# Output rows 16 partitions apart, one output transfer, and fewer, larger transfers for the last V, w4 and wo

## Chip, cores, metric

One core of one Trainium2 chip. The metric is device microseconds (us) of one execution, the median of several. A profile is taken of one execution of a kernel; its span is about 1.8 us shorter than the time (1333.3 us for a time of 1335.15).

## The reference

A decode step for two batches, one position each: attention over a cache of 16384 positions and 32 heads, mixed by a gate with a small MLP block.

```python
# A_x (2,1,1024); k_cache, v_cache (2,32,16384,128); everything bfloat16
q = (x @ wq).reshape(B, 1, 32, 128)
p = softmax(q . k_cache * 128 ** -0.5)           # per batch and head
a = (p . v_cache).reshape(B, 1, 4096) @ wo       # wo (4096, 1024)
# ... x1 = x + (w1, w2 part of the MLP)
b = x1 + gelu(layernorm(x1) @ w3) @ w4           # w4 (3584, 1024)
return g * a + (1 - g) * b                       # g = sigmoid(sum(x * gate_w))
```

K and V alone are 537 MB (2 x 2 x 32 x 16384 x 128 elements of 2 bytes), so the step is mostly a matter of reading HBM.

## The kernel before

Everything that is large comes through a ring of three 64 KB-per-partition buffers: K and V in 32 tiles each of 8.4 MB (two heads of one batch), the weights between them. All these loads are issued on the queue of SP, each as soon as a buffer is free. After the last V come w4 and wo, cut into pieces so that the matmuls can follow the landing:

```python
V_SPLIT_LAST = [NJ // 2, NJ // 2]        # the last V in two halves
W4_SPLIT = [7] * 4                       # 28 rows of 1024 per partition
WO_SPLIT = [4] * 6 + [2, 2, 1, 1, 1, 1]  # 32 rows per partition

def load_pieces(key, weights, split):
    # ...
    for n in split:
        nc.sync.dma_start(out=t[:, r0 : r0 + n, :], in_=src[:, r0 : r0 + n, :])
        r0 += n
```

One "row" here is one row of 1024 elements in each of the 128 partitions, 256 KB in all. The products of w4 and wo add up in one PSUM tile. Four groups of 32 partitions each hold a quarter of the 1024 output columns; in each group the two batches are in the first two partitions:

```python
def group(g):
    return slice(32 * g, 32 * g + B)              # B = 2

def add_row_product(actT, w_row, last=False):     # one row: four matmuls
    for g in range(NQ):                           # NQ = 4, QW = 256
        nc.tensor.matmul(out_acc[group(g), :], lhsT=actT,
                         rhs=w_row[:, g * QW : (g + 1) * QW],
                         start=False, stop=last, skip_group_check=True)
# ... at the very end
rows = t_tile([P, QW], BF16)
nc.vector.tensor_copy(out=rows[:], in_=out_acc[:])
for b, queue in enumerate((nc.sync, nc.scalar)):  # one transfer for each batch
    queue.dma_start(out=out[b].rearrange("s (g n) -> (s g) n", g=NQ),
                    in_=rows[b : 96 + b + 1 : 32, :])
```

The rows of w2 are loaded in three transfers: six rows per partition over all partitions, 216 rows into 12 partitions in a pattern whose slowest dimension is 3 (`WAYS, QUAD, BASE, MORE = 3, 4, 6, 18`), and the remaining 40.

## Time and profile before

| | |
|---|---|
| time, median of 3 | 1334.81 us (1334.72 to 1334.83) |
| span of the profile | 1333.3 us |
| read from HBM | 572.53 MB, 429 GB/s over the span |
| DMA engines busy | nine tenths or more in all slices but the last |
| PE, DVE busy | 60%, 57% |

From the page of the profile of the kernel before; each digit is the busy share of the 16 DMA engines in one fortieth of the span, in tenths:

```profile
span 1333.3 us, 11505 instructions
...
DMA  9999999999999999999999999999999999999998
...
HBM read 572.53 MB, written 0.00 MB: 429 GB/s over the span
```

The loads hardly pause: nine tenths of the engines' time or more in all slices but the last. An engine elsewhere that waits costs nothing unless its wait delays an issue by so long that the queue runs dry, so the time is the length of the stream plus what has to happen after its last byte. Both parts of the change act at the end, which the timeline shows. Its columns are start, duration, engine, line, operation, tiles, count, and in brackets the idle time before and what ended it:

```profile
1285.55 3.64 PE L446 MATMUL O<-Vn,PT 128*32 128x512 bf16 x32
...
1292.49 3.64 PE L446 MATMUL O<-Vn,PT 128*32 128x512 bf16 x32 [3.30 <-DMA Vn<-in_A_v_cache_dram]
...
1305.37 1.67 PE L495 MATMUL out_acc<-w,h2T 128*2 128x256 bf16 x28 [2.58 <-DMA w<-in_B_w_dram]
...
1309.61 1.66 PE L495 MATMUL out_acc<-w,h2T 128*2 128x256 bf16 x28 [2.57 <-DMA w<-in_B_w_dram]
...
1312.04 1.03 PE L495 MATMUL out_acc<-wo,Q 128*2 128x256 bf16 x16 [0.77 <-DMA wo<-in_A_wo_dram]
...
1314.47 1.02 PE L495 MATMUL out_acc<-wo,Q 128*2 128x256 bf16 x16 [1.40 <-DMA wo<-in_A_wo_dram]
...
1328.14 0.38 PE L495 MATMUL out_acc<-wo,Q 128*2 128x256 bf16 x4 [0.24 <-DMA wo<-in_A_wo_dram]
...
1328.78 0.39 PE L495 MATMUL out_acc<-wo,Q 128*2 128x256 bf16 x4 [0.25 <-DMA wo<-in_A_wo_dram]
...
1329.42 0.38 PE L495 MATMUL out_acc<-wo,Q 128*2 128x256 bf16 x4 [0.26 <-DMA wo<-in_A_wo_dram]
...
1329.85 0.42 DVE L703 CAST T<-out_acc 128x256 bf16<-128x256 f32 x1 [29.71 <-PE out_acc L495]
1330.30 0.63 SPq L705 DMA_DIRECT2D out_dram<-T  x1
1330.31 0.61 ACTq L705 DMA_DIRECT2D out_dram<-T  x1
```

PE is ahead of the loads at every step: each block of matmuls is short, and was released by a landing. Hence the starts of the blocks are the times of the landings, and their distances are what a transfer costs when the queue is full. Seven rows take 4.24 us (1309.61-1305.37), four take 2.43, one takes 0.64. Two of these give the price: a row costs (4.24-0.64)/6 = 0.60 us, and a transfer 0.64-0.60 = 0.04 us more, whatever the number of rows (all these transfers go to 128 partitions). Four rows should then take 2.44, and 2.43 were measured.

The chain of waits (start, duration, what) names the same end:

```profile
1319.55 9.83 DMA wo<-in_A_wo_dram
1329.38 0.04 issue
1329.42 0.41 PE out_acc L495 x4
1329.83 0.02 issue
1329.85 0.42 DVE T L703
```

The last row is issued 9.83 us before it lands. Its issue had to wait for an earlier piece, but the queue in front of it was full all that time, so that wait cost nothing.

### The profile page before, as it was taken

The page shows a single profiled execution, that of the slowest core. Times are in us where ns is not written, and L with a number is a line of the kernel's source. Part 1 is how long each engine was busy: PE and PEld are TensorE (multiplying, and loading weights), DVE is VectorE, ACT ScalarE, POOL GpSimd, SP SyncE. Part 2 cuts the span into 40 slices and gives each one's busy share as a digit, 9 for nine tenths or more (in the row PEclk, how much of TensorE's full clock was granted, in tenths as well). Part 3 has the DMA queues.
Part 4 walks back from the last instruction along what each step waited for, and adds up shares of the span by engine and source line. Part 5 has one row for each costly group of instructions (what it writes and reads, how often), then busy time and mean ns, then how long its engine had stood idle before and what let it go on. Part 6 is the DMA issues. An engine that isn't in the chain of part 4 may idle for free.

```text
span 1333.3 us, 11505 instructions
## 1 busy us (share of the span) xinstructions
PE 805.6 (60%) x4982; PEld 354.5 (27%) x5045; DVE 759.7 (57%) x1001; ACT 27.2 (2%) x68; POOL 12.8 (1%) x40
## 2 busy tenths in 40 slices
PE   2577655766556755556665555566655556665564
PEld 1223222332225322222222222222222222222231
DVE  1677665475652665555666555566655556666540
ACT  0000000000000000000000000000000000000000
POOL 0000000000000000000000000000000000000000
PEclk9788777787777777788887777888777788877775
DMA  9999999999999999999999999999999999999998
GB/s 410 439 437 433 423 437 431 427 434 431 439 428 441 431 423 437 441 437 425 433 437 431 433 433 437 433 431 437 435 429 433 437 437 425 435 435 433 431 421 337
DMA packets 12377, 573.27 MB, mean 430 GB/s; under 512 B 1384, under 2 KB 1392, under 8 KB 2203
## 3 DMA queue, kind: packets, MB, share of 16 engines
q1 hardware_dynamic: 12313, 572.53, 99.4%
q8 instruction: 39, 0.64, 0.2%
q14 instruction: 11, 0.09, 0.0%
q10 hardware_dynamic: 14, 0.01, 0.0%
HBM read 572.53 MB, written 0.00 MB: 429 GB/s over the span
## 4 chain that ended last, share of the span: by engine, by line
PE 31%; DVE 30%; DMA 23%; another core or an unknown queue 12%; issue 2%; ACT 1%; ACTq 0%; SPq 0%; DVEq 0%
DVE T L388 23%; PE S L402 20%; DMA Kn<-in_A_k_cache_dram 13%; PE O L446 7%; DMA wt<-in_B_w_dram 4%; DMA Vn<-in_A_v_cache_dram 3%; DMA wo<-in_A_wo_dram 3%; PE misc L255 2%; DVE Os L461 2%; ACT Pr L430 1%; DVE PT L434 1%; PE misc L604 1%; PE misc L585 1%; DVE mx L423 1%
## 5 line engine op out<-in xcount | busy, mean ns | idle before, releaser
L402 PE MATMUL S<-T,z 128*128 128x512 bf16 x1985 | 583.6, 423 | 323.7 <-DVE T L388 304.5
L388 DVE STREAM_TRANSPOSE T<-Kn 128x1024 f32<-128x1024 f32 x512 | 612.0, 1229 | 252.5 <-DMA Kn<-in_A_k_cache_dram 199.1
L402 PEld LDWEIGHTS <-z 128*128 128x128 bf16 x2048 | 211.2, 104 | 682.8 <-issue 521.5
L446 PE MATMUL O<-Vn,PT 128*32 128x512 bf16 x2048 | 121.4, 390 | 3.3 <-DMA Vn<-in_A_v_cache_dram 3.3
L446 PEld LDWEIGHTS <-PT 128*32 128x32 bf16 x2048 | 74.3, 140 | 49.2 <-issue 20.4
L457 DVE TENSOR_SCALAR Os<-O,xmask 128x128 f32<-128x128 f32 x32 | 11.2, 351 | 101.3 <-PE O L446 101.3
L255 PE MATMUL misc<-rs,ones_f 128*128 128x2 f32 x64 | 17.9, 350 | 79.1 <-DVE rs L477 79.1
L430 ACT ACTIVATE Pr<-S,nb 128x512 bf16<-128x512 f32 x32 | 22.0, 687 | 1198.9 <-DVE nb L425 1161.1
L469 PE MATMUL misc<-asel,Os 128*128 128x2 f32 x64 | 12.4, 264 | 50.9 <-DVE Os L461 50.9
L413 DVE TENSOR_REDUCE m<-S 128x1 f32<-128x512 f32 x32 | 22.1, 692 | 36.9 <-PE S L402 36.9
L434 DVE STREAM_TRANSPOSE PT<-Pr 128x512 bf16<-128x512 bf16 x32 | 22.8, 711 | 28.7 <-ACT Pr L430 28.7
L255 PEld LDWEIGHTS misc<-rs,ones_f 128*128 128x128 f32 x64 | 16.2, 314 | 83.9 <-issue 81.2
L461 DVE SCALAR_TENSOR_TENSOR Os<-O,xmask,Os 128x128 f32<-128x128 f32 x96 | 33.7, 351 | 3.4
L469 PEld LDWEIGHTS misc<-asel,Os 128*128 128x128 f32 x64 | 9.7, 192 | 65.2 <-DVE Os L461 61.0
L255 PE MATMUL misc<-mdiag,ones_f 128*128 128x128 f32 x64 | 15.5, 325 | 17.1 <-DVE mdiag L416 17.1
L423 DVE TENSOR_REDUCE mx<-misc 64x1 f32<-64x64 f32 x64 | 14.2, 222 | 19.1 <-PE misc L255 18.7
L362 POOL TENSOR_TENSOR z<-qsel,own 128x32 bf16<-128x32 bf16 x32 | 10.7, 333 | 1197.9 <-PE S L402 1168.1
L604 PE MATMUL misc<-xn2T,wt 128*128 128x2 bf16 x224 | 14.4, 202 | 8.0 <-DMA wt<-in_B_w_dram 8.0
L481 DVE RECIPROCAL rinv<-misc 128x2 f32<-128x2 f32 x32 | 5.5, 171 | 22.7 <-PE misc L255 22.7
L703 DVE CAST T<-out_acc 128x256 bf16<-128x256 f32 x1 | 0.4, 425 | 29.7 <-PE out_acc L495 29.7
L604 PEld LDWEIGHTS <-wt 128*128 128x128 bf16 x224 | 14.3, 169 | 8.2 <-DMA wt<-in_B_w_dram 8.2
L484 DVE SCALAR_TENSOR_TENSOR OT<-misc,g_bc,rinv 128x2 bf16<-128x2 f32 x32 | 7.0, 220 | 15.6 <-PE misc L469 15.6
(90 smaller groups left out, 122.3 us busy)
## 6 DMA issues: line engine op xcount, KB each, us to landing
Vn<-in_A_v_cache_dram SPq DMA_DIRECT2D x2, 4096.0 KB, 42.8
wt<-in_B_w_dram SPq DMA_DIRECT2D x1, 7168.0 KB
w<-in_B_w_dram SPq DMA_DIRECT2D x4, 1792.0 KB, 31.6
wo<-in_A_wo_dram SPq DMA_DIRECT2D x6, 1024.0 KB, 34.1
wt<-in_B_w_dram SPq DMA_DIRECT2D x1, 2048.0 KB, 37.3
wt<-in_B_w_dram SPq DMA_DIRECT2D x1, 1536.0 KB, 40.9
wo<-in_A_wo_dram SPq DMA_DIRECT2D x2, 512.0 KB, 18.8
wo<-in_A_wo_dram SPq DMA_DIRECT2D x4, 256.0 KB, 13.7
```

What stands on the lines that cost most here:

```text
L255: nc.tensor.matmul(ps[:], lhsT=ones_f[:], rhs=src, start=True, stop=True)
L388: moved = nc.vector.transpose(out=T[:].rearrange("p w j s -> p j w s"), in_=Kw[:, m * CW : (m + 1) * CW].rearrange("p (j w e) -> p j w e", ...
L402: nc.tensor.matmul(S[:], lhsT=z[:, v, NM - 1 - m : NM - 1 - m + P], rhs=Tb[:, v // 2, :, v % 2], start=(m == 0 and v == 0), stop=(m == NM ...
L413: nc.vector.reduce_max(out=m[:], in_=S[:], axis=AX.X)
L423: nc.vector.reduce_max(out=mx[pa, :], in_=mall[pa, pa], axis=AX.X)
L430: nc.scalar.activation(out=Pr[:], in_=S[:], func=ACTF.Exp, bias=nb[:], scale=scale, accum_out=rs[:])
L434: nc.vector.transpose(out=PT[:], in_=Pr[:])
L446: nc.tensor.matmul(O[32 * g : 32 * g + 32, :], lhsT=PT[:, m : CJ * 32 : 16], rhs=V[:, j0 : j0 + 4, :], start=(m == 0), stop=(m == NM - 1),)
L461: nc.vector.scalar_tensor_tensor(out=Os[:], in0=Ox, scalar=xmask[:, x : x + 1], in1=Os[:], op0=ALU.mult, op1=ALU.add,)
L469: nc.tensor.matmul(oc[:], lhsT=Os[:], rhs=asel[:], start=True, stop=True)
L585: nc.tensor.matmul(ps[group(g), :], lhsT=actT[rows, r, :], rhs=w[rows, r, g * HW : (g + 1) * HW], start=False, stop=(n == len(slots) - 1), ...
L604: nc.tensor.matmul(ps[:, c, :], lhsT=w[:, r, :].rearrange("k (p c) -> k p c", c=C)[:, :, c], rhs=actT[:, r, :], start=(r == 0), stop=(r == ...
```

## The change

The intent: the rows of the two batches are put 16 partitions apart, so that all eight output rows (4 groups x 2 batches) lie at one stride and leave in a single transfer, and the last loads are cut into fewer, larger pieces: 10 in place of 18. To have the second batch 16 columns on, the weights of the products get 17 columns with zeros between, which costs a memset and writes at a stride in three places, and for w4 (`h2`) a copy that was not there before.

```diff
-    V_SPLIT_LAST = [NJ // 2, NJ // 2]
# ... load_v: the last V in one transfer, as the others
-    W4_SPLIT = [7] * 4
-    WO_SPLIT = [4] * 6 + [2, 2, 1, 1, 1, 1]
+    W4_SPLIT = [14, 14]
+    WO_SPLIT = [8, 8, 8, 4, 2, 1, 1]
# ...
+    APART = 16
+    def apart(shape, dtype):
+        t = t_tile(shape + [APART * (B - 1) + 1], dtype)
+        nc.vector.memset(t[:], 0.0)
+        return t
+    def rows_of(g):
+        return slice(32 * g, 32 * g + APART * (B - 1) + 1)
     def add_row_product(actT, w_row, last=False):
         for g in range(NQ):
             nc.tensor.matmul(
-                out_acc[group(g), :],
+                out_acc[rows_of(g), :],
# ... the same in start_out; res, Q and h2 are made by apart() and filled with [:, :, ::APART]
-    for b, queue in enumerate((nc.sync, nc.scalar)):
-        queue.dma_start(
-            out=out[b].rearrange("s (g n) -> (s g) n", g=NQ), in_=rows[b : 96 + b + 1 : 32, :]
-        )
+    nc.sync.dma_start(
+        out=out.rearrange("b s (g n) -> g (b s) n", g=NQ), in_=rows[0 : P : APART, :]
+    )
```

More of the change, by code (lines that the diff above doesn't have):

```diff
@@ L114, in load_v @@
         t = big_tile("Vn")
-        tv = t[:].rearrange("p (j d) -> p j d", d=Dh)
-        src = cache_rows(A_v_cache, i)
-        j0 = 0
-        for n in V_SPLIT_LAST if i == NT - 1 else [NJ]:
-            nc.sync.dma_start(out=tv[:, j0 : j0 + n, :], in_=src[:, j0 : j0 + n, :])
-            j0 += n
+        nc.sync.dma_start(
+            out=t[:].rearrange("p (j d) -> p j d", d=Dh), in_=cache_rows(A_v_cache, i)
+        )
         vn_tiles[i] = t
@@ L506, in start_out @@
             zero_rows(out_acc, g, QW)
-        res = const.tile([P, KC, B], FP32, name="cen")
-        nc.vector.tensor_tensor(out=res[:], in0=x1, in1=over_r(omg_bc[:]), op=ALU.mult)
+        res = apart([P, KC], FP32)
+        nc.vector.tensor_tensor(
+            out=res[:, :, ::APART], in0=x1, in1=over_r(omg_bc[:]), op=ALU.mult
+        )
         for c in range(KC):
@@ L511, in start_out @@
                 nc.tensor.matmul(
-                    out_acc[group(g), c:QW:KC],
+                    out_acc[rows_of(g), c:QW:KC],
                     lhsT=res[:, c, :],
@@ L527, in wo_stage @@
         nc.tensor.matmul(q_ps[:], lhsT=perm[:], rhs=Q1[:], start=True, stop=True)
-        Q = const.tile([P, B, 32], BF16)
-        nc.vector.tensor_copy(out=Q[:], in_=q_ps[:])
+        Q = apart([P, 32], BF16)
+        nc.vector.tensor_copy(out=Q[:, :, ::APART], in_=q_ps[:].rearrange("p b r -> p r b"))
         wo = wt.pop("wo")
         for r in range(32):
-            add_row_product(Q[:, :, r], wo[:, r, :], last=(r == 31))
+            add_row_product(Q[:, r, :], wo[:, r, :], last=(r == 31))
     def layernorm(src, dst):
@@ L650, in st_down @@
         w4 = wt.pop("w4")
+        h2 = apart([P, FC], BF16)
+        nc.vector.tensor_copy(out=h2[:, :, ::APART], in_=h2T[:])
         for r in range(FC):
-            add_row_product(h2T[:, r, :], w4[:, r, :])
+            add_row_product(h2[:, r, :], w4[:, r, :])
     extra = {
@@ L703 @@
     nc.vector.tensor_copy(out=rows[:], in_=out_acc[:])
-    for b, queue in enumerate((nc.sync, nc.scalar)):
-        queue.dma_start(
-            out=out[b].rearrange("s (g n) -> (s g) n", g=NQ), in_=rows[b : 96 + b + 1 : 32, :]
-        )
+    nc.sync.dma_start(
+        out=out.rearrange("b s (g n) -> g (b s) n", g=NQ), in_=rows[0 : P : APART, :]
+    )
 _INS = ['A_x', 'A_k_cache', 'A_v_cache', 'A_wq', 'A_wo', 'B_x', 'B_w1', 'B_w2', 'B_w3', 'B_w4', 'gate_w']
```

## The prediction

> **What bounds the kernel.** The page's DMA row stands at nine tenths or more in every slice but the last (8); 572.53 MB come from HBM at 429 GB/s over the 1333.3 us span. The kernel is one stream of loads; PE (60%) and DVE (57%) have room. What the change does to them in mid-kernel (a memset and wider weights for the residual, near 267 us) is hidden while loads stay queued. Only the length of the stream and what follows its last byte count.
>
> **The tail before.** In the timeline the matmuls on w4 start as pieces land: 1301.13, 1305.37, 1309.61 us (7 rows, 4.24 apart); those on wo at 1312.04, 1314.47, 1316.89 (4 rows, 2.43 apart); the last at 1328.14, 1328.78, 1329.42 (1 row, 0.64 apart). So a row costs (4.24-0.64)/6 = 0.60 us and a transfer 0.04 us. From 1322 us the DMA moves about 300 GB/s, not 430: the packets show four of 16 engines finished, while twelve last to 1329. The cutting doesn't cause that; I expect it to stay. The DMA queue's waits for earlier pieces (8.6 us in the wo issues) cost nothing: the last issue, at 1319.55, is 9.83 us ahead of its landing.
>
> After that landing (1329.38): four matmuls 0.41, cast 0.42, two output issues at 1330.30 (0.63 on SP, 0.61 on ACT; an undisturbed load issue takes 0.33), end 1333.3.
>
> **What the change does.**
> 1. Eight transfers fewer (18 to 10 from the last V on): 8 x 0.04 = about 0.35 us off the stream, all on the critical path. No bytes are saved. The Trainium skill ("DMA: Bandwidth & Descriptors", Anatomy of one DMA) gives a single DMA about 2 us of fixed cost, mostly completion latency; with the queue full it overlaps, and 0.04 us agrees with its remark that the semaphore write is almost free.
> 2. The last V feeds PE whole: 64 matmuls (3.64 us per 32 at the tail's clock of 0.50) from 1292.4 to about 1299.8, 3.6 us later. The second w4 piece lands near 1309.5 and needs 3.3 us, the first wo piece near 1314.2: hidden.
> 3. Wider weights (17 columns for 2), two memsets, strided copies: under 2 us of DVE, hidden. An 8-row wo piece needs 2.05 us of PE against 4.8 us between landings; the last pieces are still single rows.
> 4. One output transfer of eight 512 B rows for two of four. The two issues seem to disturb each other; SP's landed 0.28 us after ACT's. Alone I expect 0.3 us less, between none and 0.5.
>
> **Predicted**: 1334.81 - 0.35 - 0.3 = 1334.15 us, range 1333.0 to 1335.1. Faster by over 2%: 0.01; within 2%: 0.98; slower by over 2%: 0.01.
>
> **What the profile would show.** Step 1: last wo landing near 1329.0 (before 1329.38), 8-row pieces about 4.85 us apart. Step 2: the last V's matmuls as one block of 7.3 us; no wo product waits for PE. Step 3: the last row product starts at its landing and takes 0.4 us. Step 4: one issue of about 0.35 us, and 2.6 to 2.9 us from its start to the span's end (3.0 before).
>
> **What would make it wrong.** An instruction fetch (16 KB, about 0.9 us on one DMA engine) falling on the slowest engine rather than another, up to 1 us either way; the transposes' buffers, now shared with the residual, delaying a load so far that the queue drains near 270 us; a slower descriptor pattern for the output; PE ordered so that w4's products hold up wo's.

## The result

Ratios in this document are the mean time of one kernel's runs over that of the other's of the same rounds, so they are not quite the ratios of the medians that are quoted.

| | before | after |
|---|---|---|
| median of 6 | 1334.72 us (1334.65 to 1334.83) | 1334.23 us (1334.12 to 1334.47) |
| ratio, 95% interval | | 0.9996 (0.9983 to 1.0009) |

The interval contains 1. Still, the slowest of the six runs after is faster than the fastest of the six before. The medians differ by 0.49 us; 0.65 were predicted.

From the page of the profile after:

```profile
span 1332.4 us, 11498 instructions
...
DMA  9999999999999999999999999999999999999998
...
HBM read 572.53 MB, written 0.00 MB: 430 GB/s over the span
```

The timeline after, the same places:

```profile
1292.13 5.94 PE L442 MATMUL O<-Vn,PT 128*32 128x512 bf16 x64 [7.09 <-DMA Vn<-in_A_v_cache_dram]
...
1309.25 3.16 PE L502 MATMUL out_acc<-w,T 128*17 128x256 bf16 x56 [5.32 <-DMA w<-in_B_w_dram]
...
1314.09 1.89 PE L502 MATMUL out_acc<-wo,T 128*17 128x256 bf16 x32 [1.68 <-DMA wo<-in_A_wo_dram]
...
1318.93 1.89 PE L502 MATMUL out_acc<-wo,T 128*17 128x256 bf16 x32 [2.95 <-DMA wo<-in_A_wo_dram]
...
1328.21 0.29 PE L502 MATMUL out_acc<-wo,T 128*17 128x256 bf16 x4 [0.22 <-DMA wo<-in_A_wo_dram]
...
1328.84 0.29 PE L502 MATMUL out_acc<-wo,T 128*17 128x256 bf16 x4 [0.34 <-DMA wo<-in_A_wo_dram]
...
1329.18 0.42 DVE L714 CAST T<-out_acc 128x256 bf16<-128x256 f32 x1 [28.02 <-PE out_acc L502]
1329.63 0.66 SPq L715 DMA_DIRECT2D out_dram<-T  x1
```

Each block of row products is still released by a landing, so PE is still ahead. Eight rows now take 4.84 us (1318.93-1314.09), which is 8 x 0.60 + 0.04. The chain of waits after ends the same way:

```profile
1300.91 27.89 DMA wo<-in_A_wo_dram
1328.80 0.04 issue
1328.84 0.31 PE out_acc L502 x4
1329.15 0.02 issue
1329.18 0.42 DVE T L714
```

The two profiles differ by 0.96 us (spans 1333.34 and 1332.37 us), more than the medians. The profiled execution of before took 1335.15 us, 0.43 more than its median in the table, and that of after 1334.15. In the profile the last V is already there 0.36 us earlier (1292.13 against 1292.49), of which the merging of V's halves explains 0.04. So this much of the difference is scatter of one execution, and a gain of half a microsecond must be read from distances inside a trace, and from medians, not from one span.

### The profile page after: what moved, and what is told of

Its sections match the earlier page's. It is cut to its first block, busy times and chain, and to the rows that moved or that the text cites. A ratio compares the mean times of both kernels' runs of the same rounds, so it can differ in the third digit from the quotient of the medians.

```text
span 1332.4 us, 11498 instructions
## 1 busy us (share of the span) xinstructions
PE 797.2 (60%) x4982; PEld 354.1 (27%) x5045; DVE 760.4 (57%) x1005; ACT 27.2 (2%) x68; POOL 12.8 (1%) x40
## 4 chain that ended last, share of the span: by engine, by line
PE 33%; DVE 30%; DMA 21%; another core or an unknown queue 12%; issue 3%; ACT 1%; ACTq 0%; SPq 0%; DVEq 0%
DVE T L384 23%; PE S L398 21%; DMA Kn<-in_A_k_cache_dram 14%; PE O L442 7%; DMA wt<-in_B_w_dram 4%; DMA wo<-in_A_wo_dram 2%; PE misc L251 2%; DMA w<-in_B_w_dram 2%; DVE Os L457 2%; ACT Pr L426 1%; DVE PT L430 1%; PE misc L613 1%; DVE mx L419 1%; PE misc L594 1%
```

## The experiments

The times are medians, each beside runs of the kernel before on the same chip (1334.81 us in the first set of four, 1334.91 in the second, nine runs each). All eight kernels gave the right result.

| kernel | us | less kernel before | ratio, 95% interval |
|---|---|---|---|
| output part only | 1334.49 | -0.32 | 0.9998 (0.9984 to 1.0012) |
| loads part only | 1334.40 | -0.41 | 0.9998 (0.9985 to 1.0010) |
| changed kernel, w4 and wo in single rows | 1337.05 | +2.24 | 1.0018 (1.0006 to 1.0031) |
| changed kernel, output issued from ACT | 1334.17 | -0.64 | 0.9996 (0.9983 to 1.0008) |
| before, again | 1334.80 | -0.11 | 1.0000 (0.9986 to 1.0014) |
| after, again | 1334.17 | -0.74 | 0.9995 (0.9982 to 1.0007) |
| changed kernel, wo in four pieces of 8 rows | 1335.61 | +0.70 | 1.0006 (0.9992 to 1.0020) |
| changed kernel, w2 dealt to seven engines | 1338.08 | +3.17 | 1.0024 (1.0010 to 1.0037) |

For differences this small the intervals don't decide; the traces must. Three figures were read from each of them: when PE began on the last of V (its landing), the distance from there to the start of the last row's products (the length of the w4 and wo stream), and the time from the first output issue to the end of the span.

| kernel | V there | V to last row | output issue to end |
|---|---|---|---|
| before | 1292.49 | 36.93 | 3.03 |
| before, again | 1292.65 | 36.93 | 3.02 |
| output part only | 1292.10 | 36.97 | 2.75 |
| loads part only | 1292.15 | 36.85 | 3.02 |
| after | 1292.13 | 36.71 | 2.75 |
| after, again | 1292.25 | 36.50 | 2.74 |
| output issued from ACT | 1292.27 | 36.43 | 2.71 |

### Only the output part

```diff
 # the changed kernel, with the cuts of before
-    W4_SPLIT = [14, 14]
-    WO_SPLIT = [8, 8, 8, 4, 2, 1, 1]
+    W4_SPLIT = [7] * 4
+    WO_SPLIT = [4] * 6 + [2, 2, 1, 1, 1, 1]
 # and the last V in two halves
```

> Only the output part of the change (rows 16 apart, one output transfer); the loads are cut as before. Theory A (output 0.3 us, eight transfers fewer 0.2 to 0.35 us, additive): 0.25 to 0.35 us less than before, and 2.7 to 2.8 us from the output issue to the end of the span against 3.03 before. Rival B (the whole gain of 0.5 us is the stream's, the rest scatter): within 0.1 us of before, about 3.0 us after the issue. In both the last wo landing lies where it did relative to the last V's landing (36.9 us after it).

Measured: 0.32 us less than before. V to last row is 36.97 us, as before; from the output issue to the end 2.75 us pass in place of 3.03. This is what theory A expects, in both numbers.

### Only the loads part

```diff
 # the kernel before
-    V_SPLIT_LAST = [NJ // 2, NJ // 2]
+    V_SPLIT_LAST = [NJ]
-    W4_SPLIT = [7] * 4
-    WO_SPLIT = [4] * 6 + [2, 2, 1, 1, 1, 1]
+    W4_SPLIT = [14, 14]
+    WO_SPLIT = [8, 8, 8, 4, 2, 1, 1]
```

> Only the coarser cuts of the last V, w4 and wo; output in two transfers as before. Theory A: 0.2 to 0.35 us less than before, the last wo landing 36.6 to 36.7 us after the last V's landing (36.9 before). Rival B: 0.5 us less. Rival C (transfers are free when the queue is full): within 0.1 us of before, 36.9 us between the landings.

Measured: 0.41 us less than before, between the numbers of A and B. In the trace V to last row is 36.85 us, outside A's 36.6 to 36.7, and by itself too near to C's 36.9 to decide. The four kernels with the coarse cuts average 36.62 (36.85, 36.71, 36.50, 36.43), the three with the fine cuts 36.95 (36.93, 36.93, 36.97): 0.33 us less, and no overlap. But the four differ among themselves by 0.42, more than that, and the five times of this run (1334.23 to 1334.83 us) reach into those of before, so the size of this part rests on the averages. Behind V seven transfers are saved (16 to 9), and 7 x 0.044 is 0.31. The output takes 3.02 us from its issue, as before. So the two parts are separate and add up: 0.33 plus 0.28 is 0.61, against 0.49, 0.74 and 0.64 us measured for both together.

### Single rows: many more transfers

```diff
-    W4_SPLIT = [14, 14]
-    WO_SPLIT = [8, 8, 8, 4, 2, 1, 1]
+    W4_SPLIT = [1] * 28
+    WO_SPLIT = [1] * 32
```

> The changed kernel with w4 and wo in 60 transfers of one row each (9 in the changed kernel, so 51 more). Theory A (0.04 us for each transfer on each DMA engine): 51 x 0.044 = 2.2 us slower than the changed kernel, about 1.7 us slower than before; row products follow each other 0.64 us apart all through the tail. Rival D (the cost is per packet, about 9 ns of a packet's time beyond its bytes: per engine 480 packets instead of 72): 3.7 us slower than the changed kernel. Rival C (free): within 0.2 us of the changed kernel. Rival E (the issues, at 0.4 us each and eight in flight, starve the engines): 5 us or more.

Measured: 2.88 us slower than the same kernel with nine transfers (1337.05 against 1334.17 of the ACT variant in the same rounds), 0.056 us for each of the 51. Theories C and E are out. A's sum was 0.7 too low, D's 0.8 too high, so the sum alone doesn't choose between them. The timeline shows the distances:

```profile
1313.60 0.39 PE L502 MATMUL out_acc<-wo,T 128*17 128x256 bf16 x4 [0.23 <-DMA wo<-in_A_wo_dram]
1314.24 0.39 PE L502 MATMUL out_acc<-wo,T 128*17 128x256 bf16 x4 [0.25 <-DMA wo<-in_A_wo_dram]
1314.92 0.39 PE L502 MATMUL out_acc<-wo,T 128*17 128x256 bf16 x4 [0.29 <-DMA wo<-in_A_wo_dram]
1316.67 0.39 PE L502 MATMUL out_acc<-wo,T 128*17 128x256 bf16 x4 [1.36 <-DMA wo<-in_A_wo_dram]
1317.23 0.40 PE L502 MATMUL out_acc<-wo,T 128*17 128x256 bf16 x4 [0.17 <-DMA wo<-in_A_wo_dram]
...
1331.94 0.39 PE L502 MATMUL out_acc<-wo,T 128*17 128x256 bf16 x4 [0.21 <-DMA wo<-in_A_wo_dram]
```

From 1316.67 to 1331.94 there are 24 rows, 0.636 us each: the 0.60 of a row and 0.036 for its transfer. The 15 rows from 1305.22 to 1314.92 took 0.647 each. D needs 0.68 (8 packets of 84 ns, as the packet records give them, and 9 for the semaphore), so its size is wrong. That the price is one for each transfer, as A has it, does not follow, though: every transfer here brings each engine eight packets (one for each of its partitions), and a price of 5 ns for a packet would give the same times.

The starts in the packet records tell the two apart. On the engine that ends last in this trace, packets of 2 KB start 80 ns apart, and from a semaphore write to the next packet 6 ns pass: 8 x 80 + 6 = 646 ns for a transfer. In the trace of the changed kernel packets of 28 KB start 1059 ns apart. So 2 KB of data take (1059-80)/13 = 75.3 ns, and a packet takes 4.7 ns beyond its data. Of the 0.044 us of a transfer about 0.038 lie with its eight packets and 0.006 with its semaphore write. A has the right price for such a transfer, and D the right kind of cost at twice its size, because the records of two successive packets overlap by 4 ns. Cutting a load by rows costs time here mainly because it cuts its packets.

What A lacks of the total lies in two places of this trace. Between 1314.92 and 1316.67 stands one gap of 1.75 us in place of 0.64; an instruction fetch of 16 KB starts just before it, at 1314.63 us, and takes 0.95 us. In the other traces a fetch stands at 1315 to 1318 us too, and the next landing is late by 0 to 0.4 us. And from the output issue to the end 3.22 us pass in place of 2.74. Both together make 1.6 us in this profile, whose execution was also 0.8 us slower than the median of the timed ones; how much of them each timed run has is open.

### The output from ACT

```diff
-    nc.sync.dma_start(
+    nc.scalar.dma_start(
         out=out.rearrange("b s (g n) -> g (b s) n", g=NQ), in_=rows[0 : P : APART, :]
     )
```

> The changed kernel with its single output transfer issued from ACT in place of SP. Theory F (the two output transfers of before delayed each other): same as the changed kernel within 0.1 us, landing 1.7 us after the issue. Rival G (SP's path is the slow one, ACT's landed 0.28 us sooner before): 0.2 to 0.3 us less than the changed kernel, landing 1.45 us after the issue.

Measured: 1334.17 us, the same as the changed kernel (1334.17 in the second set of runs). The record of landings has the single transfer landing 1.70 us after its issue from ACT, and 1.74 after its issue from SP in the changed kernel. In the kernel before, ACT's landed after 1.67 and SP's after 1.96; in its second trace, 1.67 and 1.95. So SP isn't the slower path. Of two transfers at once one lands as early as it would alone, and the other 0.28 us after it. That is theory F. The packet records show where the time goes: SP's packets start 1.53 us after the issue beside ACT's and 1.30 us when alone, and each takes only 25 to 35 ns. So the delay comes before the data move; what causes it there is not shown.

The issues themselves tell nothing of it: 0.66 us for the single one from SP, 0.62 from ACT, and 0.63 and 0.61 for the two.

### Before and after, again

> The kernel before, unchanged, as a control. Same time within 0.15 us; the scatter of its second trace shows how far one profile can be trusted: I expect the landings of the last K and V to differ by up to 0.4 us from the first trace (1272.98 and 1292.44 us), though nothing differs, because they also differ in the traces of the kernels whose loads up to there are the same.

Measured: 1334.80 us. The last K landed 0.32 us later than in the first trace (1253.99 against 1253.68; the 1272.98 of the text above is the landing of the V before the last), and the last V was there 0.16 us later (1292.65). The output part only has the same loads up to there as these two, and V at 1292.10: a scatter of 0.55 us, a little more than the 0.4 expected. The profiled execution took 1335.28 us, the slowest of its runs. The distance from V to the last row is the same in both to 0.01 us.

> The changed kernel, unchanged, beside the others of this call. Theory A (sum of both parts): 0.5 to 0.65 us less than before.

Measured: 0.74 us less than before, a little over the 0.65 expected at most. The slowest run (1334.43) is again faster than the fastest of before (1334.73).

### wo in pieces of eight rows

```diff
-    WO_SPLIT = [8, 8, 8, 4, 2, 1, 1]
+    WO_SPLIT = [8, 8, 8, 8]
```

> The changed kernel with wo in four transfers of eight rows: three transfers fewer, but the last one brings eight rows. Theory A with exposed tail: the stream ends 0.12 us sooner, but 32 matmuls (1.9 to 2.05 us) follow the last landing in place of four (0.3 to 0.4): 1.4 to 1.6 us slower than the changed kernel. Rival (only the number of transfers counts): 0.1 us faster.

Measured: 1.44 us slower than the changed kernel (1335.61 against 1334.17). In the timeline the products of the last piece start no later than those of the changed kernel's last row (1328.72 us, against 1328.84 and 1328.75 in its two traces), but they are 32 matmuls in place of four:

```profile
1323.88 1.88 PE L502 MATMUL out_acc<-wo,T 128*17 128x256 bf16 x32 [2.98 <-DMA wo<-in_A_wo_dram]
1328.72 1.89 PE L502 MATMUL out_acc<-wo,T 128*17 128x256 bf16 x32 [2.96 <-DMA wo<-in_A_wo_dram]
...
1330.66 0.42 DVE L714 CAST T<-out_acc 128x256 bf16<-128x256 f32 x1 [29.11 <-PE out_acc L502]
1331.11 0.66 SPq L715 DMA_DIRECT2D out_dram<-T  x1
```

So the coarse cut is right only up to the last rows. The change keeps 4, 2, 1, 1 there, and this is worth 1.4 us, about four times the 0.33 that its fewer transfers bring.

### w2 on seven engines: a try at the idle engines

The DMA engines don't end together. Before, in the stretch from 1280 to 1332 us (40 slices of 1.3 us):

```profile
DMA  9998999979999999999999999999999977776200
GB/s 454 479 403 361 402 424 391 510 340 441 441 419 443 386 452 419 416 454 405 477 399 405 410 447 429 410 429 435 406 413 433 422 332 303 307 307 263 84 0 3
```

After, the same:

```profile
DMA  9989999898999999899899999999999967775000
GB/s 403 454 353 391 441 435 441 356 441 375 397 419 529 419 388 419 359 545 410 388 400 413 441 416 466 429 416 403 447 419 405 418 296 299 301 301 205 9 0 3
```

For the last 7 us only three quarters of the engines move data. The record of each engine's landing shows four engines ending about 7 us before the last, in every trace with this w2, and twelve within 2 us of each other. Before w2, at 237 us, the 16 are within 1.8 us (2.2 in the second trace); the w2 transfer of 216 rows then puts three engines 5.5 us behind the first four, and over the rest of the kernel nine others lose their lead over those three. That goes with the instruction fetches (39 of 16 KB, whose records last 0.9 to 1.1 us each). No record here names the engine of a fetch, but the landings can be laid beside the fetches. In the seven traces of the second table, from 260 to 1290 us, take each engine's lag behind the first three at one large load after another. Where no fetch falls between two loads (155 times), the ordered lags repeat within 0.18 us, with a median of 0.04. Where one 16 KB fetch does (159 times), the sum of the lags grows by 1.5 us in the median. So each fetch sets engines outside the leading group back. The try was to give w2's extra rows to seven engines, in the hope that the next four are the idle ones:

```diff
-    WAYS, QUAD, BASE, MORE = 3, 4, 6, 18
+    WAYS, QUAD, BASE, MORE = 7, 4, 4, 17
```

> The changed kernel with the load of w2 dealt otherwise: fewer of its rows to all 16 engines (4 per partition in place of 6), the rest in a transfer that seven engines share in place of three. In the traces so far, twelve engines end the stream 0 to 2 us apart and four end 7 us before them, since the w2 transfer at about 250 us puts 5.5 us on three engines and instruction fetches eat up the lead of nine others, but not of four. If those four are the engines next in number to the three (theory H), the twelve end about 1.2 us sooner and the four about 4 us later: 1.0 to 1.3 us faster than the changed kernel, 1.5 to 1.9 less than before. If they are others (theory I), four of the fetching engines get 4 us more: 2 to 3.5 us slower.

Measured: 3.9 us slower than the changed kernel. The uneven transfer does land in seven steps in place of three, but at the end three engines are nearly 5 us behind the next group, while three that were early still are, by 12 us. So theory H is wrong, and theory I right in kind and a little too low in size. The Trainium skill ("DMA: Bandwidth & Descriptors", section "Why a DMA increments its semaphore by 16 and not by 1") says that a transfer on fewer than 16 engines uses as many as the largest number up to 16 that divides the slowest dimension on both sides, and the lowest-numbered of them; the three and seven landings agree with the count, as do ten and twelve for the remaining 40 and 36 rows of w2, three and seven of which come late. If the early engines are the same ones in both kernels, the result says that three of the four are not among the lowest seven. By this rule such a transfer can't reach them without also loading busy engines. No version that beats the changed kernel came of this, and the imbalance stays as it was.

## Why the prediction was right

- **The bound** was right. The page shows the stream full before and after. The memset and the wider weights of the residual had moved to 256.7 to 263.5 us in the trace, and the DMA share from 240 to 300 us was 1.02 both times.
- **Step 1, transfers**: 0.35 us predicted for eight. Measured 0.33 for the seven behind V, from the distance between V and the last row, and 0.41 us in time for this part alone; the eighth, the merging of V's halves, was not measured by itself. The prediction took the 0.04 us as a price of the transfer; the packet records put most of it on the packets (4.7 ns each). The sum is the same because every transfer here has eight packets on each engine. The last landing came at 1328.80 us, not at 1329.0; that absolute figure rests on one execution's scatter and confirms nothing.
- **Step 2, the last V whole**: hidden, as predicted. It is one block of 64 matmuls, 5.94 us and not 7.3, because the granted clock during the block (1292.13 to 1298.07 us) was 0.61 on average and not 0.50: 5.94 x 0.61 = 3.62, about the same as 7.28 x 0.50 = 3.64. The products of w4's second piece started at its landing (1309.25), and no wo product waited for PE.
- **Step 3, wider weights**: right. The last row's four products took 0.39 us in all traces but one (0.29 in the first after). The exposed rest behind the last landing did not grow.
- **Step 4, one output transfer**: 0.3 us predicted, 0.28 measured between issue and end, and 0.32 in time for this part alone. One sign of it was wrong: I expected the issue to fall to 0.35 us, taking it that the two issues got in each other's way. It takes 0.62 to 0.66 us with or without a second one. What the second transfer delayed was its own landing.
- **The dangers named** (a drained queue near 270 us, a slower pattern, PE held up) did not come. The fourth, instruction fetches, is there as scatter. It is the likely reason why single traces differ by some tenths, which is argued and not shown.
- **What the total can't tell**: the stated range (1333.0 to 1335.1 us) also holds the time of before, so the time alone would have agreed with no gain at all. What speaks for the prediction is that its two parts were measured apart.

The Trainium skill's page "DMA: Bandwidth & Descriptors" (section "Anatomy of one DMA") puts a fixed cost of about 2 us on a single DMA, mostly the wait for completion; it gives this for transfers issued from GpSimd, a path that this kernel doesn't use and that the prediction didn't mention. In this trace the single output transfer has such a latency (1.74 us), and the loads don't: with others queued behind each, all but 0.04 us is overlapped. An estimate from the page's figure alone, 2 us for each of eight transfers, would have been a gain of 16 us.

## What to carry to other kernels

In a stream that keeps the DMA engines full, a transfer more or fewer costs some hundredths of a microsecond, which the distances between landings of different sizes give directly (here mostly 4.7 ns for each of its packets); cut finely only at the very end, where the size of the last piece decides how much compute is exposed. What follows the last byte is serial, so every step there counts in full: two output transfers at once ended 0.28 us later than one. When an effect is smaller than the scatter of one execution, measure distances inside several traces and separate the parts, because a difference of two spans mixes the effect with the scatter.

## What the Trainium skill lacked or had wrong

- "DMA: Bandwidth & Descriptors" gives the fixed cost of a DMA by itself and calls the semaphore write about one cycle; it has no figure for one more transfer in a full queue. Here it is 0.036 to 0.044 us for each transfer of 128 partitions over 16 engines (4.24, 2.43 and 0.64 us for 7, 4 and 1 rows; 0.636 us a row over 24 single rows). Of this, 6 ns stand between the semaphore write and the next packet.
- The same page, section "Issuing engines are not separate DMA queues", says that transfers issued from several engines interleave and that this only saves sequencer time. It has no figure for two small stores to HBM issued from SP and ACT at the same moment, which made one of them late: 1.95 us from issue to landing against 1.67 for the other and 1.70 to 1.74 for a single one.
- "Runtime: NRT & Kernel Launch", section "Instruction fetch mechanics", calls the cost of crossing a 16 KiB block mostly hidden. It doesn't say what a fetch does to loads. Here 39 fetches of 16 KB fall into a full stream, and where one does, the engines' lags behind the first three grow by 1.5 us in sum (median of 159); the engines end some 7.4 us apart. What this costs the kernel's time is not shown, since no run has fewer fetches.
